# Reloading an activation tile through the DMA crossbar transpose instead of transposing it on TensorE

## The chip, the core and the metric

The kernel runs on one core of a Trainium2 chip. The metric is the device time of one execution, in microseconds (us). The core has five engines that run side by side: TensorE (PE, matmuls; its weight loads are listed as PEld), VectorE (DVE), ScalarE (ACT), GpSimd (POOL) and SyncE (SP), which here only issues transfers. Sixteen DMA engines move data between device memory and the on-chip memory.

## The reference

Two stages. The first is attention with 16 query heads and one shared key/value head:

```python
scores = (1 / sqrt(64)) * q @ k.T          # batch 8, 16 heads, 384 tokens, head size 64
attn   = softmax(scores)
x      = (attn @ v)                         # -> 3072 tokens x 1024
```

The second is a mixture of 16 experts in 4 groups. Each token picks a group, then an expert in that group:

```python
g_idx = argmax(x @ w_group);  g_w = softmax(...)[g_idx]          # 4 groups
e_idx = argmax(x @ w_expert[g]); e_w = softmax(...)[e_idx]       # 4 experts of the group
h   = maximum(x[tokens] @ w1[g, e], 0)                           # 1024 -> 1024
out[tokens] = g_w * e_w * (h @ w2[g, e])                         # 1024 -> 1024
```

## The kernel before

The kernel handles the 8 batches in turn (384 tokens each). For each batch it finds the expert that most of the batch's tokens chose and runs this one expert over all tokens of the batch, with a gate that is zero for the others. A (batch, expert) pair that is left after that is a leftover. For up to 32 tokens one such pair is handled at the end of the fast path, interleaved with the last batch's expert; anything more falls to a slow block that these inputs do not need.

The expert work is cut into units, and `fill(n)` puts the next n units into the instruction stream, so that TensorE has work while something else is waited for. There are eight `hps` units and six `yps` units in a batch:

```python
    def h_unit(fc):
        ...
        ps = side([P, CW], FP32, "hps")
        for ko in range(KO):
            nc.tensor.matmul(out=ps[:, 0:S], lhsT=w1[:, ko, fc * P:(fc + 1) * P], rhs=xb[:, ko, :], ...)
        nc.scalar.activation(out=state["h"][:, fc, :], in_=ps[:, 0:S], func=ACTF.Relu)

    def y_unit(st, nh):
        ...                                        # y: rows of the tag "y", three buffers
            ps = side([P, n], FP32, "yps")
            for fo in range(FO):
                nc.tensor.matmul(out=ps[:], lhsT=state["h"][:, fo, st * P:(st + 1) * P], rhs=w2[:, fo, cs], ...)
            nc.scalar.activation(out=y, in_=ps[:], func=ACTF.Copy, scale=gs_of()[:, st:st + 1])
            store(st, cs, y)                       # SyncE: rows of y to the output
```

`side` hands out PSUM tiles from one ring of three buffers. Each batch's x is written to device memory in bf16, with the 1024 features on partitions and blocks (`[128, 8, 384]`), so that the leftover batch, known only at run time, can be read back:

```python
        nc.gpsimd.tensor_copy(out=xbf[b][:, :, ts], in_=xT[b][:, :, ts])
        if st == ST - 1:
            nc.sync.dma_start(out=xb_dram[b], in_=xbf[b][:].rearrange("p k s -> p (k s)"))
```

The end of the program, with the leftover pair (cuts marked):

```python
    invert(NP - 1)
    weigh(NP - 1)                                  # ends with the store of the last batch's x
    last = B - 1
    xe = pool.tile([P, KO, S], BF16, tag="qraw", bufs=2, name="xe")
    nc.sync.dma_start(out=xe[:]..., in_=xb_dram[bass.ds(leftover["b"], 1)]...)     # L659
    fill(2)
    rest_of_gates(last)
    ...                                            # which tokens are left over: pick, pick_bf
    fill(3)
    ...
    fill(1)
    counts(None, last)
    ...
    fill(1)
    pg = side(...)                                 # gates and output rows of the leftover tokens
    ...
    fill(3)
    xtok = []
    for st in range(ST):                           # ST = 3 blocks of 128 tokens
        pb = side([P, Dm], BF16, "pb")
        for ko in range(KO):                       # KO = 8 blocks of 128 features
            nc.tensor.transpose(out=pb[:, ko * P:(ko + 1) * P], in_=xe[:, ko, st * P:(st + 1) * P], identity=ident_bf[:])   # L715
        xt = pool.tile([P, Dm], BF16, tag="pt", bufs=9, name="xt")
        nc.vector.tensor_copy(out=xt[:], in_=pb[:])                                                                       # L717
        xtok.append(xt)
        fill(1)
    px = side([P, KO, CAP], FP32, "px")            # gather: CAP = 32 tokens picked by a 0/1 matrix
    for ko in range(KO):
        for st in range(ST):
            nc.tensor.matmul(out=px[:, ko, :], lhsT=xtok[st][:, ko * P:(ko + 1) * P], rhs=pick_bf[:, st, :], ...)          # L723
    xc = pool.tile([P, KO, CAP], BF16, tag="qT", bufs=3, name="xc")
    nc.vector.tensor_copy(out=xc[:], in_=px[:])

    fill(1)
    ...                                            # ph: xc times the leftover expert's w1
    fill(1)
    ...                                            # phT: two transposes
    fill(1)
    ...                                            # py: times the leftover expert's w2 (L746)
    nc.gpsimd.indirect_dma_start(out=out4[...], ..., in_=yc[:], ...)
    fill(1)                                        # the last unit, which merges leftover rows of the last block
```

The leftover expert's weights are loaded by GpSimd-issued transfers: w1 (four pieces) during the last attention phase, w2 (L582) when the batch before the last has finished its units.

Of the kernel before, what the change touches and what calls it, by code (L numbers as in the profile page):

```python
# [10 lines left out]
BF16 = mybir.dt.bfloat16  # L11
I32 = mybir.dt.int32
U32 = mybir.dt.uint32
P = 128
# [7 lines left out]
def kernel(  # L22
# [11 lines left out]
    nc = tc.nc  # L34
    B, H, S, D = q.shape
    N, Dm = out.shape
# [5 lines left out]
    ST = S // P  # L42
    KO = Dm // P
# [10 lines left out]
    xb_dram = nc.dram_tensor("x_bf", [B, P, KO * S], BF16).ap()  # L54
# [16 lines left out]
    pool = fast.enter_context(tc.tile_pool(name="work", bufs=2))  # L71
# [4 lines left out]
    def side(shape, dtype, name):  # L76
        return ps_s.tile(shape, dtype, tag="s", name=name)

    q_raw, k_raw, v_sb, kT, qT, pt, xT, xbf, gsel, wts = {}, {}, {}, {}, {}, {}, {}, {}, {}, {}
# [90 lines left out]
    ident_bf = singles.tile([P, P], BF16, name="ident_bf")  # L170
# [258 lines left out]
    def first_units(b):  # L429
        rows = {}  # L430

        def place(st, cs):
            if cs.start == 0:
                rows[st] = pool.tile([P, Dm], FP32, tag="y", bufs=3, name="y")
            return rows[st][:, cs]

        def closes(st):
            return b == B - 1 and st == ST - 1

        def store(st, cs, y):  # L440
            if closes(st):
                if cs.start == 0:
                    leftover["row"] = y
                else:
                    nc.sync.dma_start(out=outv[b, :, st, cs], in_=y)
            elif cs.stop == Dm:
                nc.sync.dma_start(out=outv[b, :, st, :], in_=rows[st][:])

        def merge(st, cs, ps, y):
            if not closes(st) or cs.start == 0:  # L450
                return False
            if cs.start == CW:
                spread()
            nc.vector.scalar_tensor_tensor(out=y, in0=ps[:], scalar=gsel[b][:, st:st + 1], in1=leftover["y"][:, cs.start - CW:cs.stop - CW], op0=OP.mult, op1=OP.add)
            return True
        return moe_units(wts[b][0], wts[b][1], xbf[b], lambda: gsel[b], place, store, merge, lambda st, nh: 2 if closes(st) and nh == 1 else 1)
# [26 lines left out]
    def fill(n):  # L483
        while n > 0:
            if not units:
                if begun[0] >= B or begun[0] not in wts:
                    return
                units.extend(first_units(begun[0]))
                begun[0] += 1
            units.pop(0)()  # L490
            n -= 1
            ran[0] += 1
            if ran[0] == (FO + 2 * ST) * (B - 2) + FO:
                leftover_w1()
            if ran[0] == (FO + 2 * ST) * (B - 1):
                leftover_w2()
# [45 lines left out]
    leftover = {}  # L542
# [31 lines left out]
    def leftover_w1():  # L574
        leftover["e"], leftover["b"] = parts_of(leftover["reg"])
        w1 = wpool.tile([P, KO, F], BF16, tag="w1", name="w1")
        load_w1(w1, leftover["e"])
        leftover["w1"] = w1

    def leftover_w2():  # L580
        w2 = wpool.tile([P, FO, Dm], BF16, tag="w2", name="w2")
        nc.gpsimd.dma_start(out=w2[:], in_=w2f[bass.ds(leftover["e"], 1)].rearrange("a p k f -> (a p) k f"))  # L582
        leftover["w2"] = w2
    for p in range(NP):
        b, st = divmod(p, ST)
# [69 lines left out]
    invert(NP - 1)  # L655
    weigh(NP - 1)
    last = B - 1
    xe = pool.tile([P, KO, S], BF16, tag="qraw", bufs=2, name="xe")
    nc.sync.dma_start(out=xe[:].rearrange("p k s -> p (k s)"), in_=xb_dram[bass.ds(leftover["b"], 1)].rearrange("a p k -> (a p) k"))  # L659
    fill(2)  # L660
    rest_of_gates(last)
    gi = leftover["gi"]
# [25 lines left out]
    pick_bf = pool.tile([P, ST, CAP], BF16, tag="kT", name="pick_bf")  # L688
# [18 lines left out]
    nc.vector.tensor_sub(out=small[:, 1:2], in0=nfl[:], in1=small[:, 0:1])  # L707
    nex = pool.tile([1, 1], I32, tag="nex", bufs=1, name="nex")
    nc.vector.tensor_copy(out=nex[:], in_=small[0:1, 1:2])
    fill(3)  # L710
    xtok = []
    for st in range(ST):
        pb = side([P, Dm], BF16, "pb")
        for ko in range(KO):
            nc.tensor.transpose(out=pb[:, ko * P:(ko + 1) * P], in_=xe[:, ko, st * P:(st + 1) * P], identity=ident_bf[:])  # L715
        xt = pool.tile([P, Dm], BF16, tag="pt", bufs=9, name="xt")
        nc.vector.tensor_copy(out=xt[:], in_=pb[:])  # L717
        xtok.append(xt)
        fill(1)
    px = side([P, KO, CAP], FP32, "px")  # L720
    for ko in range(KO):
        for st in range(ST):
            nc.tensor.matmul(out=px[:, ko, :], lhsT=xtok[st][:, ko * P:(ko + 1) * P], rhs=pick_bf[:, st, :], start=(st == 0), stop=(st == ST - 1))  # L723
    xc = pool.tile([P, KO, CAP], BF16, tag="qT", bufs=3, name="xc")
    nc.vector.tensor_copy(out=xc[:], in_=px[:])

# [179 lines left out]
```

## Time and profile before

| | before |
|---|---|
| median of 3 runs | 460.92 us (460.87 to 461.02) |
| profiled span | 459.6 us |
| TensorE busy | 449.4 us |
| VectorE busy | 308.4 us |
| ScalarE busy | 242.0 us |
| the 24 transposes L715 | 1.8 us busy, 219 ns each |
| the three copies L717 | 2.1 us busy, 692 ns each |
| the reload of x, L659 | 7.4 us from issue to landing |

The profile is one execution. Times in its lists are counted from the start of the span. In a group's line stand the source line, the engine, the operation, the names of the output and inputs, the shape and the count; after the bar the busy time, the mean of one in ns and the engine's idle time just ahead, with what ended it. Matmuls are pipelined, so instructions of one engine overlap in the list; what one group costs the stream is seen from the starts of what follows.

### The profile page before, as it was taken

The numbers are of one execution on the slowest core, as the hardware profiler recorded it, in microseconds if no ns is written. First come the engines' busy times: TensorE is split into PE (matmuls) and PEld (weight loads), VectorE is DVE, ScalarE is ACT, GpSimd is POOL, SyncE is SP. The second block draws the span as 40 slices with busy tenths as digits, with TensorE's granted clock in tenths as the row PEclk, the third lists the DMA queues.
The fourth block names the chain that finished last, engine by engine and source line by source line (L and its number), as shares of the span: only waits on it lengthen the run. The fifth ranks groups of instructions, "written<-read, shape, count | busy, mean of one in ns | idle before, by whom it ended". The sixth has DMA issues, their size and how long they took to land.

```text
span 459.6 us, 10200 instructions
## 1 busy us (share of the span) xinstructions
PE 449.4 (98%) x4208; PEld 199.8 (43%) x4208; DVE 308.4 (67%) x488; ACT 242.0 (53%) x345; POOL 60.5 (13%) x83
## 2 busy tenths in 40 slices
PE   8999999999999999999999999999999999999893
PEld 6343445333643345433553335433454335434552
DVE  3899965499717996099843997269960999574411
ACT  2966643676337753576346773376535764542331
POOL 1004003000120113000030001200130000500000
PEclk9999999999999999999999999999999999999997
DMA  8787997996699395992979747994869910799982
GB/s 154 99 146 109 218 208 120 258 201 139 107 177 254 74 189 96 235 224 74 157 113 266 140 118 124 167 258 80 170 102 233 234 69 11 115 211 245 274 212 104
DMA packets 152454, 74.55 MB, mean 162 GB/s; under 512 B 120256, under 2 KB 138944, under 8 KB 152400
## 3 DMA queue, kind: packets, MB, share of 16 engines
q0 software_dynamic: 28416, 37.81, 48.4%
q1 hardware_dynamic: 122656, 35.68, 33.3%
q8 instruction: 35, 0.57, 0.5%
q10 hardware_dynamic: 1328, 0.33, 0.4%
q14 instruction: 19, 0.16, 0.1%
HBM read 92.62 MB, written 19.01 MB: 243 GB/s over the span
## 4 chain that ended last, share of the span: by engine, by line
PE 89%; DMA 4%; issue 2%; DVE 1%; POOL 0%; ACT 0%; ACTq 0%; SPq 0%; POOLq 0%
PE s L251 28%; PE o L290 25%; PE hps L407 16%; PE yps L417 16%; PE gps L312 2%; DMA x_bf<-xbf 2%; DMA xe<-x_bf 2%; DMA qn<-in_q_dram 1%; PE qps L228 1%; POOL xbf L301 0%; DVE presum L261 0%; PE sm L273 0%; PE pb L715 0%; DVE rinv L280 0%; DVE xT L300 0%
## 5 line engine op out<-in xcount | busy, mean ns | idle before, releaser
L253 ACT ACTIVATE pt<-s 128x1024 f32<-128x1024 f32 x144 | 142.1, 1026 | 72.3 <-PE s L251 71.5
L251 PE MATMUL s<-qT,kT 64*64 64x512 f32 x1152 | 142.7, 594 | 0.0
L290 PE MATMUL o<-pt,v 64*64 64x512 f32 x1152 | 141.1, 590 | 0.0
L261 DVE TENSOR_TENSOR presum<-presum,pt 128x1024 f32<-128x1024 f32 x96 | 116.6, 1215 | 15.2 <-ACT pt L253 9.8
L407 PE MATMUL hps<-xbf,w 128*128 128x384 bf16 x512 | 86.7, 326 | 0.0
L417 PE MATMUL yps<-w,hT 128*128 128x512 bf16 (+1 forms) x392 | 85.7, 375 | 0.0
L259 DVE TENSOR_TENSOR presum<-pt 128x1024 f32<-128x1024 f32 x24 | 29.4, 1223 | 76.8 <-ACT pt L253 75.4
L290 PEld LDWEIGHTS o<-pt,v 64*64 64x64 f32 x1152 | 43.4, 133 | 76.8 <-issue 73.0
L251 PEld LDWEIGHTS s<-qT,kT 64*64 64x64 f32 x1152 | 40.8, 133 | 66.8 <-issue 60.0
L301 POOL CAST xbf<-xT 128x1024 bf16<-128x1024 f32 x24 | 25.0, 1043 | 302.8 <-DVE xT L300 302.8
L407 PEld LDWEIGHTS <-w 128*128 128x128 bf16 x512 | 48.2, 98 | 37.6 <-issue 6.5
L419 ACT ACTIVATE y<-yps,gsel 128x512 f32<-128x512 f32 x47 | 32.3, 688 | 58.8 <-PE yps L417 57.2
L408 ACT ACTIVATE hT<-hps 128x384 bf16<-128x384 f32 x64 | 31.3, 489 | 52.1 <-PE hps L407 48.0
L417 PEld LDWEIGHTS <-hT 128*128 128x128 bf16 x392 | 37.6, 98 | 44.1 <-issue 2.4
L145 POOL DMA_DIRECT2D w<-in_moe_w_dram x36 | 24.8, 708 | 58.2 <-DVE gsel L395 45.0
L300 DVE TENSOR_TENSOR xT<-o,rinv 128x1024 f32<-128x1024 f32 x24 | 29.2, 1215 | 2.5 <-PE o L290 2.5
L280 DVE STREAM_TRANSPOSE rinv<-rc 128x1024 f32<-128x1024 f32 x24 | 29.9, 1246 | 0.8
L265 DVE TRANSPOSE_TENSOR_REDUCE fold<-presum 128x32 f32<-128x1024 f32 x24 | 29.6, 1232 | 0.0
L243 DVE STREAM_TRANSPOSE qT<-qraw 128x1024 f32<-128x1024 f32 x20 | 23.6, 1202 | 0.0
L209 ACT ACTIVATE qraw<-qraw 128x1024 f32<-128x1024 f32 x21 | 22.0, 1048 | 0.0
L273 PEld LDWEIGHTS sm<-fold,sel 64*64 64x64 f32 x192 | 7.3, 133 | 13.3 <-issue 13.3
L371 ACT ACTIVATE ex<-dl 128x60 f32<-128x60 f32 x8 | 2.0, 253 | 20.1 <-DVE dl L369 20.1
(152 smaller groups left out, 162.0 us busy)
## 6 DMA issues: line engine op xcount, KB each, us to landing
w<-in_moe_w_dram POOLq DMA_DIRECT2D x36, 512.0 KB, 11.5
w<-in_moe_w_dram POOLq DMA_DIRECT2D x9, 2048.0 KB, 26.0
out_dram<-y SPq DMA_DIRECT2D x23, 512.0 KB, 6.9
qraw<-in_q_dram SPq DMA_DIRECT2D x56, 192.0 KB, 3.7
x_bf<-xbf SPq DMA_DIRECT2D x8, 768.0 KB, 3.9
v<-in_v_dram SPq DMA_DIRECT2D x16, 96.0 KB, 3.1
k<-in_k_dram SPq DMA_DIRECT2D x28, 48.0 KB, 2.7
qn<-in_q_dram SPq DMA_DIRECT2D x4, 256.0 KB, 5.2
```

Source lines behind the costliest of these rows:

```text
L251: nc.tensor.matmul(out=ps[64 * c:64 * c + 64, a, :], lhsT=kT[b][r, j * D:(j + 1) * D], rhs=qT[p][r, c * CW:(c + 1) * CW], start=True, stop ...
L253: nc.scalar.activation(out=t[:], in_=ps[:], func=ACTF.Exp, scale=scale)
L259: nc.vector.tensor_add(out=presum[p][:], in0=pt[p, 0][:], in1=pt[p, 1][:])
L261: nc.vector.tensor_add(out=presum[p][:], in0=presum[p][:], in1=pt[p, j][:])
L265: nc.vector.tensor_reduce(out=fold[p][:], in_=presum[p][:].rearrange("p a (n i) -> p (a n) i", i=32), axis=AX, op=OP.add, apply_transpose= ...
L280: nc.vector.transpose(out=t[:].rearrange("p (b i) -> p b i", i=32), in_=rc[:].rearrange("p c b -> p (c b)").unsqueeze(2).to_broadcast([P, ...
L290: nc.tensor.matmul(out=o_ps[p][64 * a:64 * a + 64, c, :], lhsT=v_sb[b][r, j, :], rhs=pt[p, j][r, a, :], start=(j == 0), stop=(j == KB - 1))
L300: nc.vector.tensor_mul(out=xT[b][:, :, ts], in0=o_ps[p][:].rearrange("p c (h n) -> p (c h) n", n=P), in1=rinv[p][:].rearrange("p (h n) -> ...
L407: nc.tensor.matmul(out=ps[:, 0:S], lhsT=w1[:, ko, fc * P:(fc + 1) * P], rhs=xb[:, ko, :], start=(ko == 0), stop=(ko == KO - 1))
L408: nc.scalar.activation(out=state["h"][:, fc, :], in_=ps[:, 0:S], func=ACTF.Relu)
L417: nc.tensor.matmul(out=ps[:], lhsT=state["h"][:, fo, st * P:(st + 1) * P], rhs=w2[:, fo, cs], start=(fo == 0), stop=(fo == FO - 1))
L419: nc.scalar.activation(out=y, in_=ps[:], func=ACTF.Copy, scale=gs_of()[:, st:st + 1])
```

## The change

The edit loads the leftover batch's x already transposed. The transfer on SyncE's queue becomes a crossbar transpose. It reads the same bf16 block `[128 features, 8 x 384]` and writes tokens onto partitions: `xtok[:, ko * 3 + st, :]` holds 128 tokens x 128 features. This is the layout that the gather matmuls `px` take as weights. The 24 TensorE transposes and the three VectorE copies out of PSUM go away. The filler units that stood between them are kept, all ahead of `px`. The purpose is to take work from TensorE and to need the reloaded x later than before.

```diff
     last = B - 1
-    xe = pool.tile([P, KO, S], BF16, tag="qraw", bufs=2, name="xe")
-    nc.sync.dma_start(out=xe[:].rearrange("p k s -> p (k s)"), in_=xb_dram[bass.ds(leftover["b"], 1)].rearrange("a p k -> (a p) k"))
+    xtok = pool.tile([P, KO * ST, P], BF16, tag="qraw", bufs=2, name="xtok")
+    nc.sync.dma_start_transpose(out=xtok[:], in_=xb_dram[bass.ds(leftover["b"], 1)].rearrange("a p k -> (a p) k"))
     fill(2)
...
-    fill(3)
-    xtok = []
-    for st in range(ST):
-        pb = side([P, Dm], BF16, "pb")
-        for ko in range(KO):
-            nc.tensor.transpose(out=pb[:, ko * P:(ko + 1) * P], in_=xe[:, ko, st * P:(st + 1) * P], identity=ident_bf[:])
-        xt = pool.tile([P, Dm], BF16, tag="pt", bufs=9, name="xt")
-        nc.vector.tensor_copy(out=xt[:], in_=pb[:])
-        xtok.append(xt)
-        fill(1)
+    fill(6)
     px = side([P, KO, CAP], FP32, "px")
     for ko in range(KO):
         for st in range(ST):
-            nc.tensor.matmul(out=px[:, ko, :], lhsT=xtok[st][:, ko * P:(ko + 1) * P], rhs=pick_bf[:, st, :], start=(st == 0), stop=(st == ST - 1))
+            nc.tensor.matmul(out=px[:, ko, :], lhsT=xtok[:, ko * ST + st, :], rhs=pick_bf[:, st, :], start=(st == 0), stop=(st == ST - 1))
```

## The prediction

> **What bounds the kernel now.** I read the page from the top, then the waits and the order of time around the edited lines. First the busy times and the chain that ended last:
>
> ```profile
> PE 449.4 (98%) x4208; PEld 199.8 (43%) x4208; DVE 308.4 (67%) x488; ACT 242.0 (53%) x345; POOL 60.5 (13%) x83
> ...
> PE 89%; DMA 4%; issue 2%; DVE 1%; POOL 0%; ACT 0%; ACTq 0%; SPq 0%; POOLq 0%
> ```
>
> TensorE is busy for 98% of the span and carries 89% of the chain. Only what shortens its instruction stream, or its few gaps, can shorten the kernel. The chain's 4% of DMA has two entries late in the kernel. They are the store of the last batch's x and the reload of the leftover batch's x:
>
> ```profile
> 420.40 7.56 DMA x_bf<-xbf
> 428.08 7.36 DMA xe<-x_bf
> ```
>
> The load waits on the store's completion: the SyncE queue's own waits give 7.1 us of the load's line on that store. The store is issued at 420.40 and lands 7.56 us later, the load is issued at 428.08 and lands at 435.44. Now TensorE in order of time from there (start, duration, instruction; in brackets the idle time ahead and what ended it):
>
> ```profile
> 430.18 4.06 PE L407 MATMUL hps<-xbf,w 128*128 128x384 bf16 x24
> 435.49 0.62 PE L715 MATMUL pb<-ident_bf,xe 128*128 128x128 bf16 x8 [1.24 <-DMA xe<-x_bf]
> 435.94 1.46 PE L407 MATMUL hps<-xbf,w 128*128 128x384 bf16 x8
> 437.24 0.61 PE L715 MATMUL pb<-ident_bf,xe 128*128 128x128 bf16 x8
> 437.69 1.89 PE L417 MATMUL yps<-w,hT 128*128 128x512 bf16 x8
> 439.42 0.61 PE L715 MATMUL pb<-ident_bf,xe 128*128 128x128 bf16 x8
> 439.86 1.89 PE L417 MATMUL yps<-w,hT 128*128 128x512 bf16 x8
> ```
>
> TensorE runs dry once, for 1.24 us, because xe has not landed. Then three groups of eight transposes stand between three filler units. After that the stream goes on without a gap to the last yps at 452.33, and 7.3 us of eviction, store and closing follow. So this stretch is on the path, nanosecond for nanosecond. The VectorE copies L717 are not:
>
> ```profile
> L717 DVE COPY xt<-pb 128x1024 bf16<-128x1024 bf16 x3 | 2.1, 692 | 7.4 <-PE pb L715 7.4
> ```
>
> VectorE idles 7.4 us ahead of them, and the third ends at 440.75, before TensorE reaches px at 441.59.
>
> [...] The trace has 219 ns for one transpose, and they overlap: a group of eight costs far less than 8 x 219. [...] The kernel before holds no crossbar transpose[...]. [...] The trace agrees at least that the load shares the engines: 0.75 MB took 7.36 us, while the engines were full in every slice from 427 to 443.
>
> **The change part by part.**
>
> Removed from TensorE: 24 transposes. What they cost on the path is the start of the next unit less the start of the group: 435.94 - 435.49 = 0.45, 437.69 - 437.24 = 0.45, 439.86 - 439.42 = 0.44, together 1.34 us. From VectorE: three copies of 0.692 us, worth nothing as shown. Also three PSUM tiles of the shared three-buffer ring, which nobody waits for here.
>
> Moved: the three filler units that stood between the transposes now run first, as one block of six. TensorE comes to the end of the first three at 430.18 + 4.06 = 434.24, as before. It no longer needs x there, so it goes on with one hps unit (437.24 - 435.94 = 1.30) and two yps units (439.42 - 437.69 = 1.73, 441.59 - 439.86 = 1.73). It reaches px at 434.24 + 4.76 = 439.00. Before, px started at 441.59. The gain is 2.6 us: 1.24 of the wait and 1.34 of the transposes, if the transposed x has landed by 439.00. That is 10.9 us after its issue, which keeps its place: the built order of SyncE's instructions differs only in this one DMA, so it still waits for the store and goes out near 428.08. 460.9 - 2.6 = 458.3 us is the clean case.
>
> Added: one transposing DMA of 768 KB. Deadline 10.9 us, break-even at 441.59 - 428.08 = 13.5 us. Its duration must be an estimate. In the trace the SyncE-issued queue (q1) has 122656 packets, mean 291 bytes, in 33.3% of 16 engines' time. That is 0.333 x 16 x 459.6 / 122656 = 20 ns per packet. If the transpose reads each row in pieces of 128 elements, 256 bytes, it has 3072 pieces, 192 per engine, 3.8 us of engine time. The plain load's share: between 427 and 446 the queue used 31.8% of 19 us for 2.33 MB, so 0.79 MB cost 2.0 us. If only this term grows, the landing takes 7.4 + 1.8 = 9.2 us. If sharing stretches all of it in proportion, 7.4 x 3.8 / 2.0 = 14 us. The deadline lies between these, nearer the good end[...].
>
> There is a second deadline. The leftover expert's second weight matrix is issued at 425.17 and needs 20.5 us:
>
> ```profile
> L582 POOL DMA_DIRECT2D w<-in_moe_w_dram x1: 885/885/885, 425.2 to 425.2; - x1
> ...
> DMA to landing us min/median/max: 20.5/20.5/20.5
> ```
>
> So it lands at 445.7. Its first user is py, at 448.67 before, with 3.0 us to spare. In the clean case py moves up to 446.1 and 0.4 us is left. Since the DMA engines are full until about 445, each microsecond that the transpose costs them beyond the plain load delays this landing by about the same. With the 1.8 us worked out above py would wait some 1.4 us, which takes the gain down to 1.2 us, 459.7 us. I take a middle between clean and this: 459.3 us.
>
> **The rivals.**
>
> 1. The transpose is slow and px becomes the wait. For it: [...] 256-byte pieces that take turns with the weight load. [...] At twice the plain landing, 14.7 us, px would start at 442.8 and the time be about 462.
>
> 2. The weight load takes over as the wait. For it: only 0.4 us of slack, and full DMA engines. Against: nothing if the transpose costs no more engine time than the copy. This would make 458.7 to 460.
>
> 3. Nothing moves, because the row stores go out behind the transpose on the same queue and y's buffers (three) come free late. The stores issued from 428.54 took up to 13.0 us, so the second is down at about 441.9. The evictions that need those buffers come at 441.6 and 444.4 in the clean case. The first of these needs the first store only, of 9.6 us, down at 438.1, so 2.5 to 3.5 us are left. It would take a transpose that holds the queue for that long. Then the time is 459 to 461.
>
> 4. The removed work was hidden anyway. Against: TensorE has no gap after 435.49 up to its end, so the 1.34 us cannot have been hidden. I give this little.
>
> **Range and chances.** The best that the edit can do is 2.6 us of 460.9, 0.6%. A gain over 2% (9.2 us) has no source. A loss over 2% needs px to start 9.2 us later than before, at 450.8, so a landing 22.7 us after issue, three times the plain load's. I give about 45% to a landing before the deadline, 20% to one between deadline and break-even, 20% to one up to 22.7 us, 15% beyond. From this: 459.3 us, eight times in ten between 458.0 and 469. The range leans upward because gains are capped and the transpose's duration is not.
>
> **What would show it right or wrong.** Right: no TensorE idle time put down to the reload at 434 to 436; the hps unit and two yps units back to back from 434.24; px near 439.0 with no wait on xtok; landing of xtok under 10.9 us; py near 446 with at most a microsecond of wait on the second weights. Wrong in the first step: a wait of TensorE's weight load at px on the DMA xtok<-x_bf, whose length is then the landing less 10.9 us. Wrong in the second: an idle time ahead of py, with the weight load's landing grown beyond 20.5 us. If the issue of the transpose on SyncE's queue takes microseconds rather than the 0.365 us of the plain load, look at the stores after it and at the evictions L419. If the store of x_bf lands later or earlier than 428 the whole stretch shifts, and none of that is the edit's.

## The result and the profile after

The changed kernel takes 467.11 us (median of 6 runs, 465.5 to 467.61), against 460.99 us (460.87 to 461.27) for the kernel before in the same measurement. The ratio is 1.0127, with a 95% interval from 1.0112 to 1.0142: 6.1 us slower. The change moved work off TensorE as intended, and lost more by waiting. Measured again later, it was 465.94 us at a ratio of 1.0117 (1.0100 to 1.0134).

The profiled execution has a span of 465.1 us, 5.5 us more than before. Busy times and the chain that ended last, of the changed kernel:

```profile
PE 450.2 (97%) x4184; PEld 199.5 (43%) x4184; DVE 306.2 (66%) x485; ACT 241.9 (52%) x345; POOL 60.4 (13%) x83
...
PE 89%; DMA 5%; issue 2%; DVE 1%; POOL 0%; ACT 0%; POOLq 0%; SPq 0%; ACTq 0%
```

TensorE has 24 instructions fewer and 0.8 us more busy time. The DMA share of the chain grew from 4% to 5%. The end of the chain in order of time (start, duration, step) says which transfer:

```profile
420.69 7.54 DMA x_bf<-xbf
428.28 17.31 DMA xtok<-x_bf
446.46 3.24 PE yps L417 x8
```

The reload takes 17.31 us, against 7.36 us for the plain load before, and the yps unit behind px takes 3.24 us, where such a unit took 1.73. The instructions in order of time, of the changed kernel, TensorE and SyncE's queue:

```profile
428.28 15.29 SPq L659 DMA_TRANSPOSE xtok<-x_bf  x1
...
430.48 5.36 PE L407 MATMUL hps<-xbf,w 128*128 128x384 bf16 x32
...
435.68 3.62 PE L417 MATMUL yps<-w,hT 128*128 128x512 bf16 x16
...
443.68 9.92 SPq L447 DMA_DIRECT2D out_dram<-y  x4
445.64 0.82 PE L714 MATMUL px<-pick_bf,xtok 128*128 128x32 bf16 x24 [6.34 <-DMA xtok<-x_bf]
446.30 3.40 PE L417 MATMUL yps<-w,hT 128*128 128x512 bf16 x8
449.62 1.06 PE L723 MATMUL ph<-w,xc 128*32 128x256 bf16 x32
```

The kernel before, from px on:

```profile
441.59 0.75 PE L723 MATMUL px<-pick_bf,xt 128*128 128x32 bf16 x24
442.19 1.89 PE L417 MATMUL yps<-w,hT 128*128 128x512 bf16 x8
444.01 1.06 PE L732 MATMUL ph<-w,xc 128*32 128x256 bf16 x32
```

The six filler units run back to back from 430.48, and TensorE is out of work at 445.64 - 6.34 = 439.30. Then it waits 6.34 us for the transpose. The span's 5.5 us come apart as follows. The filler block starts 0.3 us later than before (430.48 for 430.18), which is ahead of anything changed. From there to px it is 445.64 - 430.48 = 15.16, before 441.59 - 430.18 = 11.41: 3.75 us more. From px to ph it is 449.62 - 445.64 = 3.98, before 444.01 - 441.59 = 2.42: 1.56 us more. From ph to the start of the last yps (456.90, before 451.28) it is 7.28, before 7.27: nothing. The sum is 5.6 us.

The 1.56 us stand beside a lower clock. Busy time by stretches of 2 us of the changed kernel; the clock granted to TensorE is the third number from the end, after POOL:

```profile
440.00:442.00 2.00, 0.00 (x0) 0.00 (x0) 0.00 (x0) 0.02 (x1) 0.00 (x0) 1.00 1.20 198
442.00:444.00 2.00, 0.00 (x0) 0.00 (x0) 0.00 (x0) 0.00 (x0) 0.00 (x0) 0.64 1.23 137
444.00:446.00 2.00, 0.36 (x13) 0.37 (x14) 0.00 (x0) 0.00 (x0) 0.00 (x0) 0.50 1.18 366
446.00:448.00 2.00, 2.00 (x23) 0.90 (x20) 0.42 (x1) 0.00 (x0) 0.00 (x0) 0.50 1.02 406
448.00:450.00 2.00, 2.00 (x21) 0.78 (x23) 0.00 (x0) 0.22 (x1) 0.00 (x0) 0.65 0.36 139
```

In this run the idle time begins at 439.30. The clock falls to 0.50 at about 442.5, some 3 us later, and is back at 1.00 from about 449.4, about 4 us after px. In between lies the yps unit of 3.24 us.

### The profile page after: what moved, and what is told of

It reads as the page before. It is cut to its first block, busy times and chain, and to the rows that moved or that the text cites. A ratio compares the mean times of both kernels' runs of the same rounds, so it can differ in the third digit from the quotient of the medians.

```text
span 465.1 us, 10148 instructions
## 1 busy us (share of the span) xinstructions
PE 450.2 (97%) x4184; PEld 199.5 (43%) x4184; DVE 306.2 (66%) x485; ACT 241.9 (52%) x345; POOL 60.4 (13%) x83
## 2 busy tenths in 40 slices
DMA packets 155414, 74.55 MB, mean 160 GB/s; under 512 B 123344, under 2 KB 142032, under 8 KB 155360
## 4 chain that ended last, share of the span: by engine, by line
PE 89%; DMA 5%; issue 2%; DVE 1%; POOL 0%; ACT 0%; POOLq 0%; SPq 0%; ACTq 0%
PE s L251 27%; PE o L290 25%; PE hps L407 16%; PE yps L417 15%; DMA xtok<-x_bf 4%; PE gps L312 2%; DMA x_bf<-xbf 2%; PE qps L228 1%; PE warm L152 1%; POOL xbf L301 0%; DVE presum L261 0%; PE sm L273 0%; PE warm L474 0%; DVE rinv L280 0%; DVE xT L300 0%
## 5 line engine op out<-in xcount | busy, mean ns | idle before, releaser
L417 PE MATMUL yps<-w,hT 128*128 128x512 bf16 (+1 forms) x392 | 87.0, 379 | 0.0
L312 PE MATMUL gps<-xT,gw 128*32 128x96 f32 (+2 forms) x576 | 12.6, 239 | 0.0
```

## The experiments

Two explanations of the 17 us stood. Either the transpose is slow in itself: SyncE's queue is held for 15.29 us by one DMA_TRANSPOSE instruction, where the plain load held it 0.365 us. Or it is slow because it shares the DMA engines with the leftover expert's second weights (2 MB in bf16, issued at 425.46). I thought the first more likely and put it down as the theory of the first runs.

| run | time, us (median) | ratio to before, 95% interval |
|---|---|---|
| without the second weights' load | 458.94 | 0.9953 (0.9938 to 0.9968) |
| gap filled with matmuls | 466.07 | 1.0112 (1.0093 to 1.0130) |
| the same, again | 465.84 | 1.0106 (1.0089 to 1.0123) |
| changed kernel, measured with the run above | 465.94 | 1.0117 (1.0100 to 1.0134) |
| transpose issued early | 467.40 | 1.0135 (1.0118 to 1.0152) |
| plain load, a filler unit moved | 459.90 | 0.9983 (0.9975 to 0.9990) |
| plain load in 256-byte pieces | 473.13 | 1.0267 (1.0250 to 1.0284) |
| nine blocks of 24 transposed | 466.67 | 1.0120 (1.0096 to 1.0144) |
| second weights held back | 467.73 | 1.0153 (1.0124 to 1.0182) |
| half of them held back | 464.46 | 1.0075 (1.0047 to 1.0102) |

### Without the second weights' load

```diff
 def leftover_w2():
-    w2 = wpool.tile([P, FO, Dm], BF16, tag="w2", name="w2")
-    nc.gpsimd.dma_start(out=w2[:], in_=w2f[bass.ds(leftover["e"], 1)]...)
-    leftover["w2"] = w2
+    leftover["w2"] = wts[B - 1][1]
```

The leftover rows are then computed with another expert's second weights; the instructions of all engines stay, but for the issue of that load.

> The changed kernel without the load of the leftover expert's second weights; py multiplies the last batch's second weights instead, so the leftover rows are not the reference's, but every engine's instructions stay. Nothing but small stores shares the DMA engines with the transpose after about 431. Theory (SyncE's own work on the transpose, block by block, sets its time): the transpose still holds SyncE's queue for about 15 us (15.29 in the changed kernel), lands about 2 us after that, px waits about 6 us, and the time stays near 467 (465.5 to 467.5). Rival (it is slow because it shares the DMA engines with the 2 MB weight load and its queue is pushed back): the hold falls below 10 us, the landing below 11, px waits for nothing, and the time falls to 458 to 460.

My theory fell. The transpose in SyncE's queue, and px with no wait, of this run:

```profile
428.75 4.48 SPq L657 DMA_TRANSPOSE xtok<-x_bf  x1
...
439.56 0.76 PE L712 MATMUL px<-pick_bf,xtok 128*128 128x32 bf16 x24
```

The hold is 4.48 us instead of 15.29, the transfer lands 8.0 us after its issue instead of 17.3, and px comes straight after the fillers. So both the long hold and the late landing come from sharing the engines with these weights. How they prolong the hold is not shown. With the weights out of the way the change gains 0.47% (0.32 to 0.62%).

### The gap filled

```diff
     fill(6)
+    gap = side([P, CW], FP32, "gap")
+    for _ in range(27):
+        nc.tensor.matmul(out=gap[:], lhsT=ones_bf[:], rhs=wts[last][1][:, 0, 0:CW], start=True, stop=True)
     px = side([P, KO, CAP], FP32, "px")
```

> The changed kernel with 27 matmuls of 128x512 whose result nobody reads, put between the six filler units and px, about 5.9 us of TensorE work inside its 6.3 us of idle time. Theory (part of the loss is the clock, which fell to 0.5 after the idle time and came back only about 4 us after px; the yps unit behind px took 3.3 us for 1.73): the clock stays at 1.0, the unit behind px takes 1.73 us again, and the time falls by about 1.5 us to 465.5, with px at the same place, about 445.6. Rival (the slow unit is slow because the DMA traffic or an eviction holds it): the unit still takes over 3 us and the time stays at 467 or grows.

In order of time, TensorE of this run:

```profile
445.57 0.77 PE L717 MATMUL px<-pick_bf,xtok 128*128 128x32 bf16 x24 [0.62 <-DMA xtok<-x_bf]
446.18 1.89 PE L417 MATMUL yps<-w,hT 128*128 128x512 bf16 x7
448.00 1.06 PE L726 MATMUL ph<-w,xc 128*32 128x256 bf16 x32
```

px stays at its place, and ph follows after 2.43 us instead of 3.98. In the profile the lower clock's cost is thus 1.55 us, and it is gone when TensorE is kept busy: the granted clock is 1.00 throughout from 440 to 452. The device time says less: 466.07 us, 1.0 below the changed kernel, where I expected 1.5, and the two intervals of the ratio overlap. So both were run again side by side:

> The changed kernel once more, on the chip of the next run and in the same rounds, so that the two can be compared directly. It should stay between 466.5 and 467.5.

> The changed kernel with the 27 unread matmuls in TensorE's gap, again. If the lower clock behind the gap costs time, as the profile's 1.6 us between px and ph say, it is 1.2 to 1.8 us below the changed kernel beside it, and the two ranges of runs hardly overlap. If that is an effect of single executions, the two agree within 0.5 us.

The changed kernel came out at 465.94, half a microsecond below what I expected of it, and the filled one at 465.84: no difference. The traces again have 1.3 us between them from px to ph (3.75 and 2.43) and 1.1 us in the span (464.4 and 463.3). The two disagree outside the span. In all eight executions of the filled kernel, here and above, the device time exceeds the span by 2.7 to 3.1 us; in those of every other kernel here it is 1.5 to 1.6. So within the span the clock's part is shown, and the filled kernel loses about as much outside it. What it loses it to stays open.

### The transpose issued early

```diff
+    xtok = pool.tile([P, KO * ST, P], BF16, tag="qraw", bufs=2, name="xtok")
+    nc.sync.dma_start_transpose(out=xtok[:], in_=xb_dram[B - 2])
     bound_a()
     fill(2)
```

with the two lines taken out further down. It reads batch 6's x, so the leftover rows come from other tokens.

> The changed kernel with the transpose issued ahead of the last values stage, from batch 6's x, which has long been stored, instead of the leftover batch's; so the leftover rows are computed from other tokens, with the same instructions. The transpose then no longer waits for the store that lands at 428. Theory (only the late landing costs, and without it the sum of the prediction holds): the hold of about 15 us lies before 420, px starts near 439.0 with no wait, TensorE has no gap, py is near 446, and the time is 458.3, up to 459.5 if the weights for py come late. Rival (the transpose also costs something else, weight loads slowed or stores delayed): time of 460 or more with px at its place and a new wait, named by the trace.

```profile
394.91 12.22 SPq L648 DMA_TRANSPOSE xtok<-x_bf  x1
...
438.92 0.75 PE L714 MATMUL px<-pick_bf,xtok 128*128 128x32 bf16 x24
...
452.65 1.90 PE L737 MATMUL py<-w,hc 128*32 128x256 bf16 x32 [6.58 <-DMA w<-in_moe_w_dram]
```

px is where the prediction's sum puts it, at 438.92 with no wait. But the time is 467.40: py now waits 6.58 us for the second weights, which landed 27.3 us after their issue (20.5 before). Issued at 394.91 among eight weight loads of 512 KB and one of 2 MB (392.94 to 399.32), the transpose took 32.4 us to land, and those weights were late in turn: the slowest of these 512 KB loads landed after 40.9 us, against 32.2 in the changed kernel, and the second weights, issued later, go over the same queue. This was the rival, and its size surprised me.

### What the DMA engines do meanwhile

The view of the DMA queues, cut to 2 us, shows how the two transfers share the engines. The line of a queue has packets, MB, and the time its packets took as a share of 16 engines (packets overlap, so it can pass 100%); q0 carries the weights (GpSimd-issued), q1 what SyncE issues. The kernel before, from 433 to 435, with the plain load and the first row stores in flight:

```profile
q1 hardware_dynamic: 83, 0.41, 53.0%
q0 software_dynamic: 93, 0.19, 50.0%
```

The changed kernel, the same stretch:

```profile
q0 software_dynamic: 177, 0.36, 95.1%
q1 hardware_dynamic: 178, 0.05, 17.2%
```

The changed kernel from 441 to 443, when the weights run out, and from 443 to 445:

```profile
q1 hardware_dynamic: 650, 0.17, 96.2%
q0 software_dynamic: 73, 0.12, 31.6%
...
q1 hardware_dynamic: 1731, 0.49, 123.3%
q0 software_dynamic: 2, 0.00, 0.6%
```

Before, 83 packets against 93: about one for one, with some 5 KB in each of q1's, so q1 moves two thirds of the bytes. After, 178 against 177: again one for one, but q1's packets now hold 256 bytes and q0's 2 KB. The transpose gets an eighth of what the weights get. 11 turns per engine in 2 us are 180 ns a turn, of which its own piece is a small part (17.2% of the time, against 95.1%). From 427 to 441 only some 730 of its 3072 pieces went; from 443 to 445, with the weights gone, 1717 did (14 of the 1731 packets are larger, of the row stores). So here the transpose ends shortly after the weights end (445.6 and 443.6). Issued early it had time to use up its turns, 192 per engine, while weights still passed, in packets of 1 and 2 KB. From 400 to 404 and from 412 to 416 this run has:

```profile
q0 software_dynamic: 611, 0.61, 89.8%
q1 hardware_dynamic: 591, 0.15, 28.3%
...
q0 software_dynamic: 352, 0.72, 94.6%
q1 hardware_dynamic: 354, 0.09, 17.1%
```

This leaves open whether the crossbar has a part in it. The next run has none.

### The plain load in 256-byte pieces

```diff
-    xe = pool.tile([P, KO, S], BF16, tag="qraw", bufs=2, name="xe")
-    nc.sync.dma_start(out=xe[:]..., in_=xb_dram[bass.ds(leftover["b"], 1)]...)
+    xe = pool.tile([P, KO * ST, 2, P], BF16, tag="qraw", bufs=2, name="xe")
+    nc.sync.dma_start(out=xe[:, :, 0, :], in_=xb_dram[bass.ds(leftover["b"], 1)].rearrange("a p (n c) -> (a p) n c", c=P))
```

The kernel before, otherwise unchanged, with the TensorE transposes reading the spaced tile: the gaps in the destination cut the rows.

> The kernel before with its plain load, but the destination spaced so that the load goes in 3072 pieces of 256 bytes; no crossbar in it, TensorE transposes kept. Theory (what makes the transfer slow is the size of its pieces: each DMA engine takes one piece of 256 bytes and one weight packet of 2 KB in turn, about 175 of each in 2 us, until the weights are done near 443): the plain load lands 16 to 18 us after its issue, the first transposes wait about 10 us for it, and the time is about 471 to 473. Rival (the crossbar itself is slow beside other traffic): the load lands in 7 to 9.5 us and the time is 461 to 463.

The queues from 433 to 435 of this run and q1 from 441 to 443, and then TensorE's wait:

```profile
q0 software_dynamic: 176, 0.36, 94.6%
q1 hardware_dynamic: 180, 0.05, 17.4%
...
q1 hardware_dynamic: 1810, 0.46, 105.4%
```

```profile
444.98 1.03 PE L715 MATMUL pb<-ident_bf,xe 128*128 128x128 bf16 x8 [10.45 <-DMA xe<-x_bf]
```

A plain load with pieces of that size lands after 16.6 us, nearly as late as the transpose's 17.3. The crossbar is not what made the reload slow beside the weights; the size of the pieces is (180 packets of 256 bytes against 176 of 2 KB from 433 to 435). Two things differ. From 441 to 443 this load moved 1810 packets, the transpose 650: the transpose has a slow stretch of its own, whose cause is open. In the landing the two differ by 0.7 us all told. And this load held SyncE's queue for only 0.64 us, the transpose for 15.29. The long hold came with the transpose, the late landing with both.

### Nine blocks of 24 through the crossbar

```diff
-    xtok = pool.tile([P, KO * ST, P], BF16, ...)
-    nc.sync.dma_start_transpose(out=xtok[:], in_=...)
+    xe = pool.tile([P, (KO - 3) * ST, P], BF16, ...)          # 15 blocks, plain
+    nc.sync.dma_start(out=xe[:]..., in_=...[:, 3 * S:])
+    xtok = pool.tile([P, 3 * ST, P], BF16, ...)
+    nc.sync.dma_start_transpose(out=xtok[:], in_=...[:, 0:3 * S])
...
-    fill(6)
+    fill(4)                                                   # then 8 transposes, fill(1), 7 transposes, fill(1)
```

> A mix: nine of the 24 blocks through the crossbar, the other 15 by a plain load issued just ahead and TensorE transposes, four fillers ahead of them and two behind. Theory of turns: 1152 pieces are 72 per engine, one for each weight packet, about 13 us beside the weights; with the start after about 3 us and the plain part ahead of it the transpose lands about 16 us after its issue, near 444.5, hardly earlier than with all 24 blocks; px waits some 4 to 5 us and the time is 464 to 466. Rival (landing goes with the number of blocks, 9/24 of 15.3 us plus 2): it lands in about 8 us, px waits for nothing and the time is 459.2.

```profile
429.34 3.86 SPq L662 DMA_TRANSPOSE xtok<-x_bf  x1
...
445.33 0.42 PE L732 MATMUL px<-pick_bf,xtok 128*128 128x32 bf16 x9 [4.81 <-DMA xtok<-x_bf]
```

Three eighths of the pieces land after 16.0 us, against 17.3 for all. The theory of turns said about 16 and a wait of 4 to 5 us; the time, 466.67, is 0.7 above its range. Transposing less hardly helped while the weights passed. The hold of SyncE's queue is only 3.86 us here, with nearly as late a landing and the same weights beside it. So the hold was shorter with nine blocks than with 24 (3.86 us and 15.29), and it did not last until the pieces had landed (433.2 and 445.3).

### The second weights held back, all or half

A one-column GpSimd copy from xtok into the weight tile, ahead of the weights' load, makes this load wait until the transpose has landed: in the first version the transpose is down at 434.3, the copy runs at 434.50 and the load goes out at 435.75. In the second version only the second half of the load is behind that copy.

```diff
 def leftover_w2():
     w2 = wpool.tile([P, FO, Dm], BF16, tag="w2", name="w2")
+    nc.gpsimd.tensor_copy(out=w2[:, 0, 0:1], in_=leftover["xtok"][:, KO * ST - 1, 0:1])
     nc.gpsimd.dma_start(out=w2[:], in_=...)
```

> The changed kernel with the load of the leftover expert's second weights held until the transpose has landed. Theory of turns: the transpose has the engines nearly to itself after the first weights are down at about 431, lands about 8 us after its issue as it did without that load, and px starts near 439.5 with no wait. The weights then land about 12 to 14 us after 436.5, at 449 to 451, py waits 3 to 5 us for them, and the time is 461.5 to 464: the wait moves and does not go away. Rival (something of the transpose itself is slow in this place): px still waits.

```profile
438.95 0.76 PE L716 MATMUL px<-pick_bf,xtok 128*128 128x32 bf16 x24
...
453.38 1.90 PE L739 MATMUL py<-w,hc 128*32 128x256 bf16 x32 [7.28 <-DMA w<-in_moe_w_dram]
```

The transpose lands in 6.2 us and px is on time. The wait moved to py, as expected, but it is 7.28 us and not 3 to 5: the weights took 17.5 us from their issue at 435.75. The row stores account for a part of this at most: q1 moved only 38 packets from 437 to 445. The rest is open. The time is 467.73, nearly 4 us above what I gave.

> As the one before, but only the second half of those weights is held until the transpose has landed; the first half goes out at 425 as before. Theory of turns: the first half is down at about 436, until then turns are taken one for one, after that the transpose runs free and lands near 438 to 440, so px waits 0 to 1 us; the second half lands at 446 to 448, when py is at its second half, so it waits 0 to 2 us. Time 458.5 to 461. If halves do not help: 461 to 464.

```profile
440.65 0.77 PE L718 MATMUL px<-pick_bf,xtok 128*128 128x32 bf16 x24 [1.69 <-DMA xtok<-x_bf]
...
452.02 0.62 PE L741 MATMUL py<-w,hc 128*32 128x256 bf16 x16 [3.66 <-DMA w<-in_moe_w_dram]
```

Two waits, 1.69 us at px and 3.66 us at py, and 464.46 us: above my range again. The transpose landed after 12.6 us. Between 435 and 439 it had the engines almost to itself and still moved only 783 and 864 pieces in 2 us, half of what it did from 443 to 445 in the changed kernel; why is open, as with the slow stretch above. The second half of the weights took 10.1 us.

### Plain load, one filler unit moved

```diff
-    fill(3)
+    fill(4)
     xtok = []
     for st in range(ST):
         ...                       # eight transposes, copy
-        fill(1)
+        if st > 0:
+            fill(1)
```

This keeps the load and the transposes of the kernel before. It takes only the other half of the change, that x is needed later.

> The kernel before, plain load and TensorE transposes kept, with one filler unit moved from behind the first group of transposes to ahead of it (four fillers ahead instead of three). The first transpose is then reached at 435.5 instead of 434.2, and the plain load lands at 435.4. If the 1.24 us of idle time is all that is to be had from the order: 459.7 (459.5 to 460.2), no idle time put down to the reload. If something behind it absorbs the gain (the copies, the weights for py): 460.3 to 461.

```profile
430.66 5.36 PE L407 MATMUL hps<-xbf,w 128*128 128x384 bf16 x32
435.88 1.07 PE L715 MATMUL pb<-ident_bf,xe 128*128 128x128 bf16 x16
436.78 1.89 PE L417 MATMUL yps<-w,hT 128*128 128x512 bf16 x7
...
440.68 0.76 PE L724 MATMUL px<-pick_bf,xt 128*128 128x32 bf16 x24
```

The transposes follow the fourth unit with no idle time of TensorE. The time is 459.90 us, at a ratio of 0.9983 (0.9975 to 0.9990). It beats both kernels, by one moved unit. From the filler block's start px comes after 440.68 - 430.66 = 10.02 us, before after 11.41: the wait of 1.24 us is gone.

## Why the prediction was right or wrong

It said 459.3 us, with eight in ten between 458.0 and 469, and by its shares for the landing, which were my estimate, 85% for a change under 2%. The measured 467.11 lies in the range and under 2%, but the centre had the wrong sign: a gain of 1.6 us was expected, and the loss is 6.1. The range held only because it leaned upward for a slow transpose; the case that came, a landing between break-even and 22.7 us, had 20%.

**The path and what it would save: right.** The fillers were to end 4.76 us after 434.24, at 439.00. TensorE ran out at 439.30, with the block started 0.30 us later: to the hundredth. Where x was there in time, px started at 438.92 (early issue), 438.95 (weights held back) and 439.56 (no second weights, in an execution whose transpose was issued 0.67 us later). The device time of this last run, 458.94 us, is 0.6 above the clean case. The copies on VectorE were worth nothing, as said.

**The rule for the loss: right.** A landing beyond 10.9 us was to become a wait of landing less 10.9: 17.31 - 10.9 = 6.4 us, measured 6.34. Put into the prediction's sum, the clean 458.3 and this wait make 464.7 us; with the 1.56 us of the lower clock it is 466.3.

**The landing: wrong.** This is the term of the sum that was mis-sized: 17.3 us, where the prediction gave 9.2 to 14 and leaned to "the good end". The number of pieces was right, 3072 of 256 bytes: the profile of the changed kernel has 123344 packets under 512 bytes, the one before 120256, 3088 more. The mistake was to price a piece by its own time (20 ns), or to stretch the plain load's landing in proportion. Beside the weights' queue a piece here cost a whole turn, 180 ns, most of it the other queue's packet: 178 packets against 177, with 17.2% of the time against 95.1%. The numbers for it were in the profile before. From 433 to 435 it has 83 packets of the reload's queue against 93 of the weights', and this is q0, the weights' queue, from 427 to 446:

```profile
q0 software_dynamic: 1567, 2.62, 74.7%
```

That is 98 packets per engine (1567 / 16). At one turn each, 192 pieces per engine outnumber them, so the transpose had to land no earlier than about when the weights do, near 445.7: an estimate from these counts. It landed at 428.28 + 17.31 = 445.6. That the two figures meet is in part chance: in this run the weights were down at 425.46 + 18.1 = 443.6, and the rest of the pieces took 2 us more.

**The transpose beside a plain load.** With the weights passing, the plain load in large packets took 7.36 us, the plain load in pieces of 256 bytes 16.6 us, and the transpose 17.3 us. With little beside it the transpose landed in 6.2 and 8.0 us.

**The rivals.** The first, a slow transpose with px as the wait, is what happened. The ground that the prediction gave for it, 256-byte pieces that take turns with the weight load, held: 178 packets against 177. The second, the second weights taking over as the wait, did not happen in the changed kernel: there the weights landed sooner than before (18.1 us, before 20.5), and py came at 454.28, long after. It happened where px was on time: 6.58 and 7.28 us at py. The third, stores delayed behind the transpose, is half true: they were issued from 443.68 instead of 428.54, and no wait was put down to them. The fourth, hidden work, is refuted by the runs without a wait.

**What no step had:** the lower clock behind the gap, 1.56 us in the trace from px to ph. The prediction counted a wait as long as it is. In the second pair of traces it is 1.3 us.

**The full gain was not reached here.** The plain load moves its bytes in large packets (some 5 KB) and is done before the weights (435.44 against 445.7). Any order of transpose and weights that I tried left a wait at px or at py.

## What to carry to other kernels

Price a transfer by the number of its packets when another queue is busy: in these runs two queues moved about one packet each in turn, with packets from 256 bytes to 5 KB (83 against 93, 178 against 177). The crossbar transpose here, 3072 pieces of 256 bytes, landed 17.3 us after its issue, 2 us after the weight load ended; issued early it took 32.4 us, with little beside it 6.2 and 8.0. And when an edit has two parts, here a cheaper instruction stream and a later need, try the part that adds no transfer alone.

## What the runs showed of the hardware that was not expected

- One DMA_TRANSPOSE held SyncE's queue for 15.29 us beside the weights and for 4.2 and 4.5 us without them; one of nine blocks in place of 24 held it for 3.86 us beside them. A plain load of the same pieces held it for 0.64 us. The row stores behind it on that queue waited, from 428.54 in the kernel before to 443.68.
- In four stretches of three runs two queues on the DMA engines took turns one packet for one: 83 to 93 (5 KB against 2 KB), 178 to 177 and 354 to 352 (256 bytes against 2 KB), 591 to 611 (256 bytes against 1 KB).
- In the changed kernel TensorE's granted clock fell to 0.50 about 3 us into an idle time of 6.34 us and was back at 1.00 about 4 us after work resumed; with the idle time filled it stayed at 1.00.
- From 441 to 443 the transpose moved 650 pieces, a plain load in the same pieces 1810. The cause is open.
